# Attention events in order of time, and weight sums made in place at one pair in three steps

## The chip, the cores and the metric

The kernel runs on one core of a Trainium2 chip. The metric is the device time of one execution in microseconds (us), the median of several runs. Beside it stands one profiled execution, whose trace gives every instruction's start, duration and wait. The engines are named as in the profile: PE is TensorE (PEld its weight loads), DVE is VectorE, ACT is ScalarE, POOL is GpSimd, SP is SyncE, which here only issues DMAs.

## What is computed

Attention in a sliding window of 64 keys, over 8 sequences of 576 tokens with 8 heads of 64 channels, and behind it a feed-forward layer (512 to 2048 to 512) with the Mish function. All of it is float32.

```python
scores = scale * np.matmul(q, k.transpose(0, 1, 3, 2))
mask = (rel >= 0) & (rel < window)          # window = 64
scores = np.where(mask, scores, -1000000000.0)
scores = scores - np.max(scores, axis=-1, keepdims=True)
attn = np.exp(scores)
attn = attn / (np.sum(attn, axis=-1, keepdims=True) + 1e-09)
x = np.matmul(attn, v)                      # then heads side by side: 4608 x 512
h = x @ w_in
sp = np.where(h > 20.0, h, np.log1p(np.exp(np.minimum(h, 20.0))))
out = (h * np.tanh(sp)) @ w_out
```

## The kernel before

**Tiling.** The 4608 tokens are 12 chunks of 384. The attention of a chunk is four units `p`, one for each pair of heads (`NPAIR`). The feed-forward layer of a chunk is 16 steps `f` of 128 hidden channels. To keep float32 accuracy, each operand is split into a high and a low part in float32r, and each product is three matmuls (high by high, high by low, low by high). The high and low parts of the first weight lie in the tile `wi`, those of the second in `wo_h` and `wo_l`.

**Plain stage.** Chunks 0 to 3 are computed step by step (`steps`, a list of 64 pairs of chunk and `f`; indices 32 to 47 are chunk 2, 48 to 63 chunk 3). A step is twelve matmuls into `h_ps` on PE (called H below), two Mish activations on ACT (`t`, `gh`), a subtraction on POOL (`gl`), and, two steps later, nine matmuls into the three `acc` banks (called A below).

**Attention beside it.** While PE runs the steps of one chunk, the attention of a later one is put between them. For chunk 3 this is a list of events (time in half steps, kind, function, unit) that `Att.plan` fills at line 546: scores at `begin + p * step`, transposition 0.6 of a step later, values 1.5 steps later (`lag=1.5`, line 768). `run(slot)` (line 549) takes events from the front of the list while the first one is due. These lie within chunk 2's steps. A unit's path is: score matmuls into `s_ps` (PE; called S), masks (DVE, `pr<-s_ps,masks`), a table load and six exponentials (ACT, `pr<-pr,mx`), normalisation and a 32-by-32 transposition (DVE, `sm`, `pr`, `tr`), twelve DMAs that move blocks of `tr` to their place in `pT` (SP, `pT<-tr`), value matmuls into `o_ps` (PE; called O), and the split of the result on ACT (`xh`) and DVE (`xl`).

**Wide stage.** Chunks 4 to 11 are computed two at a time (`Wide`), with seven products of sums of weight blocks and activation blocks in place of eight products. Its attention (`Wide.run`, line 842) computes the values of unit `k - 1` (matmuls into `at`) beside the scores of unit `k` (into `s_ps` and `at`) in one place; `first_runs` puts runs 0 to 4 of the first pair of chunks among chunk 3's steps. Its transposed probabilities `tr` have the buffer `st0` (line 881).

**Weight sums.** For each pair `g` of hidden blocks, `make_sums` (line 788) forms four sums of weight blocks and writes them, split, to `sums` in DRAM: plain blocks are copied by DMA (lines 791, 792), `w` is the sum of the high and low parts (DVE, line 796, buffer `st0`), `s` holds the four sums (DVE, line 803, buffer `st1`), and `two` holds high and low parts of two of them at a time (ACT line 807, POOL line 808, buffers `st2` and then `st0`), from which one DMA for each two sums writes them (line 809). A manual dependency keeps the start of each behind the PE instruction that was last in program order. The loop at line 1123 calls it at steps with `n % 4 == 1`: 33, 37, ... 61. `load_sums` later brings the sums of a pair from DRAM into a ring that lies over `wi`; `Wide.fills` (line 909) splits the activation sums into slots that also lie over `wi` (ACT line 906, DVE line 907, with POOL's subtractions at line 915). `kept["u"]`, which the first product of each wide pair is copied to (ACT, line 966), has the buffer `st2`.

**What sets the order.** Each engine executes its instructions in the order of its queue. Up to step 31 the program order is kept; from there a scheduler orders the instructions of DVE, ACT, POOL and SP by dependencies and priorities when the kernel is built. SP's queue holds all loads of q, k and v, the moves `pT<-tr` and the writes of `sums`, and a DMA that waits holds up all that stand behind it.

Of the kernel before, what the change touches and what calls it, by code (L numbers as in the profile page):

```python
# [10 lines left out]
F32 = mybir.dt.float32  # L11
F32R = mybir.dt.float32r
# [3 lines left out]
ALU = mybir.AluOpType  # L16

P = 128
# [11 lines left out]
def tile_window_attn_mish_ffn(  # L30
# [10 lines left out]
    nc = tc.nc  # L41
# [15 lines left out]
    NG = NF // 2  # L57
# [51 lines left out]
    def thin_masks(engine):  # L109

        for r in range(TQ, P, BLK):
            for k in range(0, TK, TQ):
                engine.tensor_copy(all_masks[r:r + TQ, :, k:k + TQ], all_masks[r:r + TQ, :, k + TQ:k + 2 * TQ])
# [7 lines left out]
    wi = const.tile([P, NF, 2, NC_, P], F32R, name="wi")  # L121
# [12 lines left out]
    def in_order():  # L134
        return tc.issue_after(order[-1]) if order else nullcontext()
# [20 lines left out]
    def st_home(shape, dtype, name, n=None):  # L156
        return mp.tile(shape, dtype, name=name, tag=f"st{next(st_turn) if n is None else n}", bufs=1)
# [270 lines left out]
    def w_ready(piece):  # L428

        lo, hi, wh, wl = piece  # L430
        vec.tensor_scalar(lo, lo, 29, None, ALU.logical_shift_right)
        yield
        vec.tensor_scalar(hi.bitcast(F32), hi.bitcast(F32), BIG, -BIG, ALU.min, ALU.max)
        yield

    def w_joined(piece):

        lo, hi, wh, wl = piece
        vec.scalar_tensor_tensor(lo, hi, 3, lo, ALU.logical_shift_left, ALU.bitwise_or)
        yield  # L440
        vec.scalar_tensor_tensor(lo, hi, 0x80000000, lo, ALU.bitwise_and, ALU.bitwise_or)
        rounding.append(lambda copy: copy(wh, lo.bitcast(F32)))
        yield

    def w_rest(piece):
        lo, hi, wh, wl = piece
        vec.tensor_tensor(wl, lo.bitcast(F32), wh.bitcast(F32), ALU.subtract)
        w_load()
        yield
# [98 lines left out]
    events = []  # L548
    def run(slot):
        while events and events[0][0] <= slot:  # L550
            _, _, fn, p = events.pop(0)
            fn(p)
# [4 lines left out]
    def flush():  # L557
        c, f, gg = pend.pop(0)
        if f == 0:
            if c == 1:  # L560
                accs[c] = [at_bank(f"acc1_{t}", DO) for t in range(NTT)]
            else:
                accs[c] = [ps_acc.tile([P, DO], F32, name=f"acc{t}", tag=f"acc{t}") for t in range(NTT)]
        ffn_out(accs[c], gg, f)
        if f == NF - 1:
            ffn_store(c, accs.pop(c))
# [12 lines left out]
    starts = {c: 2 * len(steps) + 2 * NF * (c - 2) for c in range(2, PLAIN + 1)}  # L579
# [49 lines left out]
    def step(n, h_ps=None):  # L629
        pend.append((*steps[n], function(h_ps or first_half(n))))  # L630
# [58 lines left out]
    parts = {}  # L689
# [76 lines left out]
    ahead = 6  # L766
    begin = starts[2] + ahead - 1
    atts[3].plan(begin, (starts[3] - ahead - begin) / (NPAIR + 0.5), lag=1.5)
    begin = starts[3] - ahead

    PIECE = 2 * 2 * P
    RING = NPROD * PIECE
    sums = tc.dram_tile([NG, P, RING], F32, name="sums")
# [5 lines left out]
    def piece(g, m):  # L779

        def at(first, order="p (l k n) -> p l k n"):
            return ring[:, g % 2, first * PIECE:(first + 1) * PIECE].rearrange(order, l=2, k=2)
        if m in (A11, A12):
            both = ring[:, g % 2, :2 * PIECE].rearrange("p (l h k n) -> p l h k n", l=2, h=2, k=2)
            return both[:, :, m == A12]
        return at({S2: 2, S3: 3, A22: 4, S1: 5, S4: 6}[m])

    def make_sums(g):

        f0, f1 = 2 * g, 2 * g + 1  # L790
        kept_ = [nc.sync.dma_start(sums[g, :, :2 * PIECE], wi[:, f0].rearrange("p l c n -> p (l c n)").bitcast(F32)),
                 nc.sync.dma_start(sums[g, :, 4 * PIECE:5 * PIECE].rearrange("p (l n) -> p l n", l=2),
                                   wi[:, f1, :, 2:, :].rearrange("p l c n -> p l (c n)").bitcast(F32))]
        w = st_home([P, 2, 2, 2 * P], F32, "w", 0)
        parts = [wi[:, f0:f1 + 1, i, :, :].rearrange("p f c n -> p f (c n)").bitcast(F32) for i in range(2)]
        kept_.append(nc.vector.tensor_tensor(w.rearrange("p f h n -> p f (h n)"), *parts, ALU.add))
        for i in kept_:
            tc.add_manual_dep(i.ins, order[-1].name, SYNC, reason="the steps before it first")
        s = st_home([P, 4, 2 * P], F32, "s", 1)
        s1, s2, s3, s4 = (s[:, i, :] for i in (2, 0, 1, 3))  # L800
        for out_, a, b, op in ((s1, w[:, 1, 0, :], w[:, 1, 1, :], ALU.add), (s2, s1, w[:, 0, 0, :], ALU.subtract),
                               (s3, w[:, 0, 0, :], w[:, 1, 0, :], ALU.subtract), (s4, w[:, 0, 1, :], s2, ALU.subtract)):
            nc.vector.tensor_tensor(out_, a, b, op)
        for n, first in ((2, 2), (0, 5)):
            two = st_home([P, 2, 2, 2 * P], F32R, "two", n)
            i = slice(0, 2) if n else slice(2, 4)
            nc.scalar.copy(two[:, :, 0, :], s[:, i, :])
            nc.gpsimd.tensor_tensor(two[:, :, 1, :], s[:, i, :], two[:, :, 0, :].bitcast(F32), ALU.subtract)
            nc.sync.dma_start(sums[g, :, first * PIECE:(first + 2) * PIECE],
                              two.rearrange("p m l n -> p (m l n)").bitcast(F32))  # L810

    def load_sums(g, part):
        g %= NG
        nc.scalar.dma_start(ring[:, g % 2, part].bitcast(F32), sums[g, :, part])
# [231 lines left out]
    def weights(n):  # L1046
        for i in range(5 + (n in MORE)):
            if i == RES:
                residue()
            next(ops, None)  # L1050

    def some_moves():
        if slow:
            each, moved = slow.pop(0)
            moved.extend(itertools.islice(each, 4))

    def between(n):

        if n in SCORES:
            p = SCORES.index(n)  # L1060
            third.products(p, [h_bank("s_ps") for _ in range(2)])
            third.load(p + 2, "qk")
            with in_order():
                flush()
            third.masked(p, BY_HEAD, exps=False)
            if p % 2:
                third.exp(p - 1)
                third.exp(p)
        if n - 1 in SCORES[1::2]:
            third.normal(SCORES.index(n - 1) - 1)  # L1070
        if n - 2 in SCORES[1::2]:
            third.normal(SCORES.index(n - 2))
        if n in MOVED:
            p = MOVED.index(n)
            third.dve_transpose(p, p > 1)

    sums_made = 0
# [5 lines left out]
    def wide_runs(slot):  # L1083
        while first_runs and first_runs[0][0] <= slot:
            with in_order():
                wides[0].run(first_runs.pop(0)[1])

    for n, (c, f) in enumerate(steps):
        held[0] = n < starts[2] // 2
        if n >= starts[2] // 2 and f == 0:  # L1090

            while any(fn.__self__ is atts[c] for _, _, fn, _ in events):
                run(events[0][0])
        if n == starts[2] // 2:
            held[0] = True
            third.values(NPAIR - 1, h_bank)
            with in_order():
                flush()
            held[0] = False
        if n >= HEAD:  # L1100
            step(n)
        if n == MASKED:
            thin_masks(pool)
        run(2 * n)
        wide_runs(2 * n)
        if held[0]:
            if n not in SCORES:
                weights(n)
            if last < n < last + NPAIR:
                third.values(n - last - 1, h_bank)  # L1110
        if len(pend) > LAG:
            with in_order():
                flush()
        if held[0]:
            between(n)
            if n in SCORES:
                weights(n)
            some_moves()
            if last - 2 <= n < last:
                third.load(n - last + 2, "v")  # L1120
        run(2 * n + 1)
        wide_runs(2 * n + 1)
        if n >= starts[2] // 2 and n % 4 == 1 and sums_made < NG:
            make_sums(sums_made)
            sums_made += 1
        if c == PLAIN - 1 and f in (7, 8):
            for part in LOADS:
                load_sums(f - 7, part)
# [77 lines left out]
```

## Time and profile before

| | |
|---|---|
| Time, median of 3 runs | 945.4 us (944.63 to 946.57) |
| The profiled execution | 947.67 us, of which the span from the first to the last instruction is 945.8 us |
| PE busy | 879.3 us (93% of the span) |
| DVE, ACT, POOL busy | 440.5, 459.8, 240.1 us |
| Mean granted TensorE clock | 0.969 |

An engine is busy while an instruction of it executes; waiting in front of one is idle time, and the trace names for each idle stretch the event that came last before the instruction (its releaser). The granted clock is the share of TensorE's full rate that the chip allowed in a stretch; 1.00 and 0.50 are its two levels here (2.4 and 1.2 GHz). Times in rows are from the start of the span.

### The profile page before, as it was taken

What the parts mean: (1) busy time and instruction counts of PE and PEld (TensorE: products, weight loads), DVE (VectorE), ACT (ScalarE), POOL (GpSimd) and SP (SyncE); (2) the same over time, 40 slices, a digit from 0 to 9 for tenths busy, and PEclk for the clock granted to TensorE, in tenths of its full rate; (3) what the DMA queues carried; (4) which work ended last, traced back from release to release, by engine and by line L of the source; (5) the groups of instructions that cost most, each with busy time, mean ns of one, the idle gap of its engine ahead of it and who ended that gap; (6) DMA issues with size and microseconds to landing.
All of it is one profiled execution on the core that took longest, in us unless ns stands there. A gap on an engine that the chain in (4) does not pass through costs nothing.

```text
span 945.8 us, 18947 instructions
## 1 busy us (share of the span) xinstructions
PE 879.3 (93%) x7162; PEld 778.8 (82%) x7162; DVE 440.5 (47%) x1271; ACT 459.8 (49%) x1215; POOL 240.1 (25%) x227
## 2 busy tenths in 40 slices
PE   7899999997796887499999999999999999999998
PEld 6788888896686876478988888888888988898987
DVE  7887986332242436344245544245544244332322
ACT  6767464454552654255347455346455344332322
POOL 4400000233121235221314312315311324322221
PEclk8999999998898998699999999999999999999999
DMA  9554543452556654375555565555575543533311
GB/s 306 169 171 134 159 155 113 151 190 62 170 158 224 232 168 155 118 222 156 177 171 183 160 227 155 177 171 185 161 224 154 176 137 123 178 123 112 123 34 67
DMA packets 91771, 152.05 MB, mean 161 GB/s; under 512 B 9760, under 2 KB 72736, under 8 KB 87584
## 3 DMA queue, kind: packets, MB, share of 16 engines
q1 hardware_dynamic: 77424, 84.31, 28.1%
q10 hardware_dynamic: 14256, 66.53, 21.9%
q8 instruction: 57, 0.93, 0.4%
q14 instruction: 34, 0.28, 0.1%
HBM read 114.88 MB, written 24.12 MB: 147 GB/s over the span
## 4 chain that ended last, share of the span: by engine, by line
PE 55%; DMA 4%; DVE 4%; ACT 3%; issue 2%; SPq 2%; POOL 0%; ACTq 0%; DVEq 0%; POOLq 0%
PE acc L129 27%; PE m_ps L129 23%; DMA sums<-two 3%; PE at L129 3%; ACT pr L82 2%; DVE wi L907 2%; SPq L82 2%; PE s_ps L129 2%; DMA out<-o 1%; PE h_ps L129 1%; DVE sm L82 1%; DVE pr L82 1%; ACT xn L865 0%; DMA pT<-tr 0%; DVE tr L82 0%
## 5 line engine op out<-in xcount | busy, mean ns | idle before, releaser
L129 PE MATMUL m_ps<-wi 128*128 128x384 f32 x1152 | 221.7, 340 | 24.1 <-ACT u L966 19.7
L129 PEld LDWEIGHTS m_ps<-wi 128*128 128x128 f32 x1152 | 204.2, 189 | 37.3 <-ACT u L966 21.0
L129 PE MATMUL acc<-wo_h,gh 128*128 128x512 f32 x576 | 227.9, 400 | 7.1 <-ACT o L383 7.1
L947 POOL TENSOR_TENSOR gl<-t,gh 128x384 fp32r<-128x384 f32 x128 | 131.4, 1027 | 383.4 <-PE m_ps L129 122.5
L129 PE MATMUL acc<-wo_l,gh 128*128 128x512 f32 x576 | 226.8, 394 | 0.0
L129 PE MATMUL acc<-wo_h,gl 128*128 128x512 f32 x576 | 224.3, 392 | 0.0
L129 PE MATMUL h_ps<-xh,wi 128*128 128x384 f32 x512 | 143.3, 342 | 0.4 <-ACT pT L82 0.4
L129 PEld LDWEIGHTS acc<-wo_h,gh 128*128 128x128 f32 x576 | 108.6, 189 | 26.7 <-ACT o L383 7.5
L129 PEld LDWEIGHTS acc<-wo_h,gl 128*128 128x128 f32 x576 | 108.7, 189 | 24.9
L129 PEld LDWEIGHTS acc<-wo_l,gh 128*128 128x128 f32 x576 | 109.0, 189 | 15.5
L82 ACT ACTIVATE pr<-pr,mx 128x96 f32<-128x96 f32 (+1 forms) x288 | 105.6, 372 | 19.9 <-DVE mx L82 19.7
L942 ACT ACTIVATE gh<-t 128x384 fp32r<-128x384 f32 x96 | 50.4, 526 | 125.8 <-DVE t L959 84.9
L959 DVE TENSOR_TENSOR u<-u,m_ps 128x384 f32<-128x384 f32 x64 | 35.3, 552 | 140.2 <-PE m_ps L129 135.8
L129 PEld LDWEIGHTS h_ps<-xh,wi 128*128 128x128 f32 x512 | 95.2, 191 | 4.0 <-ACT pT L82 0.6
L959 DVE TENSOR_TENSOR t<-u,m_ps 128x384 f32<-128x384 f32 x96 | 53.1, 553 | 84.3 <-PE m_ps L129 84.3
L129 PE MATMUL h_ps<-xl,wi 128*128 128x384 f32 x256 | 87.0, 340 | 0.0
L82 POOL TENSOR_TENSOR gl<-t,gh 128x384 fp32r<-128x384 f32 x32 | 34.9, 1090 | 180.4 <-ACT gh L82 166.7
L82 DVE CUSTOM_DVE_ANT_0 pr<-s_ps,masks 128x96 f32<-128x96 f32 (+1 forms) x256 | 49.6, 259 | 62.7 <-PE s_ps L129 59.6
L82 ACT ACTIVATE t<-h_ps 128x384 f32<-128x384 f32 x64 | 31.5, 492 | 69.7 <-PE h_ps L129 67.1
L82 ACT ACTIVATION_READ_ACCUMULATOR pr<-pr,mx 128x1 f32 x288 | 55.2, 192 | 0.0
L1032 DVE TENSOR_TENSOR acc_sb<-acc_sb,acc 128x512 f32<-128x512 f32 x56 | 38.4, 686 | 34.8 <-PE acc L129 34.8
L943 ACT ACTIVATE t<-t 128x384 f32<-128x384 f32 x96 | 50.2, 525 | 8.7 <-PE m_ps L129 0.5
(72 smaller groups left out, 942.2 us busy)
## 6 DMA issues: line engine op xcount, KB each, us to landing
wi<-sums ACTq DMA_DIRECT2D x32, 1024.0 KB, 5.2
wi<-sums ACTq DMA_DIRECT2D x32, 768.0 KB, 4.8
v_t<-vN SPq DMA_DIRECT2D x46, 384.0 KB, 4.6
k_t<-kT SPq DMA_DIRECT2D x44, 224.0 KB, 5.2
pT<-tr SPq DMA_DIRECT2D x192, 48.0 KB, 3.5
q_t<-qT SPq DMA_DIRECT2D x47, 192.0 KB, 5.1
st<-w_in SPq DMA_DIRECT2D x16, 512.0 KB, 3.6
st<-w_out SPq DMA_DIRECT2D x16, 512.0 KB, 3.6
```

The source lines that it names most:

```text
L82: i = call(*args, **kw)
L129: i = nc.tensor.matmul(*args, **kw)
L907: nc.vector.tensor_tensor(low, b, high.bitcast(F32), ALU.subtract)
L942: nc.scalar.activation(gh, t, AF.Mish)
L943: nc.scalar.activation(t, t, AF.Mish)
L947: nc.gpsimd.tensor_tensor(gl, t, gh.bitcast(F32), ALU.subtract)
L959: nc.vector.tensor_tensor(out_, a, b, ALU.add)
L1032: nc.vector.tensor_tensor(total, total, acc, ALU.add)
```

## The change

It has three parts. The list of events is sorted by time and kind, so that the scores of unit `p + 1` (at 1.0 step behind those of `p`) are taken from the list ahead of the values of unit `p` (at 1.5). `make_sums` forms the four sums in the tile that holds the parts: `w` has the buffer `st1`, all four high parts go into one tile `high` in `st2` with one ACT instruction, the low parts overwrite `w` with one POOL instruction, and each of the two tiles is written with one DMA, in runs of 256 elements (1 KB) where before a run had 1024 (4 KB); two places of the ring change names accordingly. And the pairs are made at steps 33, 36, 39, ... 54.

```diff
     atts[3].plan(begin, (starts[3] - ahead - begin) / (NPAIR + 0.5), lag=1.5)
+    events.sort(key=lambda e: e[:2])
     begin = starts[3] - ahead
...
-        return at({S2: 2, S3: 3, A22: 4, S1: 5, S4: 6}[m])
+        return at({S2: 2, S3: 3, S4: 4, S1: 5, A22: 6}[m])
...
-                 nc.sync.dma_start(sums[g, :, 4 * PIECE:5 * PIECE].rearrange("p (l n) -> p l n", l=2),
+                 nc.sync.dma_start(sums[g, :, 6 * PIECE:].rearrange("p (l n) -> p l n", l=2),
                                    wi[:, f1, :, 2:, :].rearrange("p l c n -> p l (c n)").bitcast(F32))]
-        w = st_home([P, 2, 2, 2 * P], F32, "w", 0)
-        parts = [wi[:, f0:f1 + 1, i, :, :].rearrange("p f c n -> p f (c n)").bitcast(F32) for i in range(2)]
-        kept_.append(nc.vector.tensor_tensor(w.rearrange("p f h n -> p f (h n)"), *parts, ALU.add))
+        w = st_home([P, 4, 2 * P], F32, "w", 1)
+        parts = [wi[:, f0:f1 + 1, i, :, :].rearrange("p f (h k) n -> p f h (k n)", h=2).bitcast(F32) for i in range(2)]
+        kept_.append(nc.vector.tensor_tensor(w.rearrange("p (h f) n -> p f h n", h=2), *parts, ALU.add))
         for i in kept_:
             tc.add_manual_dep(i.ins, order[-1].name, SYNC, reason="the steps before it first")
-        s = st_home([P, 4, 2 * P], F32, "s", 1)
-        s1, s2, s3, s4 = (s[:, i, :] for i in (2, 0, 1, 3))
-        for out_, a, b, op in ((s1, w[:, 1, 0, :], w[:, 1, 1, :], ALU.add), (s2, s1, w[:, 0, 0, :], ALU.subtract),
-                               (s3, w[:, 0, 0, :], w[:, 1, 0, :], ALU.subtract), (s4, w[:, 0, 1, :], s2, ALU.subtract)):
+        a11, a21, a12, a22 = (w[:, i, :] for i in range(4))
+        for out_, a, b, op in ((a22, a21, a22, ALU.add), (a21, a11, a21, ALU.subtract),
+                               (a11, a22, a11, ALU.subtract), (a12, a12, a11, ALU.subtract)):
             nc.vector.tensor_tensor(out_, a, b, op)
-        for n, first in ((2, 2), (0, 5)):
-            two = st_home([P, 2, 2, 2 * P], F32R, "two", n)
-            i = slice(0, 2) if n else slice(2, 4)
-            nc.scalar.copy(two[:, :, 0, :], s[:, i, :])
-            nc.gpsimd.tensor_tensor(two[:, :, 1, :], s[:, i, :], two[:, :, 0, :].bitcast(F32), ALU.subtract)
-            nc.sync.dma_start(sums[g, :, first * PIECE:(first + 2) * PIECE],
-                              two.rearrange("p m l n -> p (m l n)").bitcast(F32))
+        high = st_home([P, 4, 2 * P], F32R, "high", 2)
+        nc.scalar.copy(high, w)
+        low = w.bitcast(F32R)
+        nc.gpsimd.tensor_tensor(low, w, high.bitcast(F32), ALU.subtract)
+        for i, part in enumerate((high, low)):
+            to = sums[g, :, 2 * PIECE:6 * PIECE].rearrange("p (m l n) -> p m l n", m=4, l=2)
+            nc.sync.dma_start(to[:, :, i, :], part.bitcast(F32))
...
-        if n >= starts[2] // 2 and n % 4 == 1 and sums_made < NG:
+        if n >= starts[2] // 2 and (n - starts[2] // 2) % 3 == 1 and sums_made < NG:
```

**First place: ACT's queue in chunk 2's steps, from the exponentials of unit 1.** ACT has one instruction for each thing that PE does there: `pr,sm<-pr,mx` (six) follows a unit's scores, `t` and `gh` follow each H, `xh<-o_ps` follows a unit's values. Before:

```order
L82 CAST xh1_2463<-o_ps_2465 128x384
L807 CAST two_2440<-s_2431 128x2x256
L82 ACT_TABLE_LOAD
L82 ACTIVATE pr_2508,sm_2510<-pr_2508,mx_2509 128x96 x6
L82 ACT_TABLE_LOAD
L82 ACTIVATE t_2566<-h_ps_2553 128x384
L82 ACTIVATE gh_2567<-h_ps_2553 128x384
L82 ACTIVATE t_2594<-h_ps_2581 128x384
L82 ACTIVATE gh_2595<-h_ps_2581 128x384
L82 CAST xh1_2463<-o_ps_2609 128x384
```

The values of unit 0 (`o_ps_2465`) stand ahead of the exponentials of unit 1, and two H lie between those and the values of unit 1 (`o_ps_2609`). In the changed kernel:

```order
L82 ACTIVATE pr_2453,sm_2455<-pr_2453,mx_2454 128x96 x6
L82 ACT_TABLE_LOAD
L82 ACTIVATE t_2497<-h_ps_2484 128x384
L82 ACTIVATE gh_2498<-h_ps_2484 128x384
L82 CAST xh1_2503<-o_ps_2505 128x384
L82 ACTIVATE t_2558<-h_ps_2545 128x384
L82 ACTIVATE gh_2559<-h_ps_2545 128x384
L82 ACT_TABLE_LOAD
L82 ACTIVATE pr_2599,sm_2601<-pr_2599,mx_2600 128x96 x6
L82 ACT_TABLE_LOAD
L82 ACTIVATE t_2647<-h_ps_2634 128x384
L82 ACTIVATE gh_2648<-h_ps_2634 128x384
```

Behind the exponentials of unit 1 now come the values of unit 0 (`o_ps_2505`) and the exponentials of unit 2; those of unit 1 stand two rows further. On PE three H, four A, the values of unit 0 and the scores of unit 2 lie between the scores and the values of unit 1.

**Second place: SP's queue at the moves of unit 3 of chunk 3.** Before:

```order
L809 DMA sums<-two 128x1024 x2
L82 DMA v_t<-vN 128x6x128
L82 DMA q_t<-qT 128x384
L82 DMA k_t<-kT 128x448
L82 DMA pT<-tr 32x192 x12
```

In the changed kernel:

```order
L82 DMA pT<-tr 32x192 x2
L82 DMA v_t<-vN 128x6x128
L82 DMA pT<-tr 32x192 x3
L810 DMA sums<-high 128x4x256
L82 DMA pT<-tr 32x192 x3
L810 DMA sums<-w 128x4x256
L82 DMA pT<-tr 32x192 x4
```

The twelve moves stood in one piece; a load of v, which waits for the values of unit 2, and both writes of a pair's sums, which wait for ACT and for POOL, now stand among them. Units 2 of chunk 3 and 1 of the first wide pair also have sums among their moves, the others none.

**Third place: DVE's queue at the end of chunk 3.** `tr` are the transposed probabilities of the next wide pair of chunks, L907 the low parts of the activation sums, `u` the first addition of the wide stage. Before:

```order
L907 TENSOR_TENSOR x_4225<-xn_3805,x_4225 128x768
L82 STREAM_TRANSPOSE tr<-pr 128x6x3x32 x2
L796 TENSOR_TENSOR w<-wi 128x1024
L803 TENSOR_TENSOR s<-w 128x256 x2
L907 TENSOR_TENSOR wi<-t_4226,wi 128x768
L803 TENSOR_TENSOR s<-s,w 128x256
L907 TENSOR_TENSOR wi<-t_4227,wi 128x768
L803 TENSOR_TENSOR s<-w,s 128x256
L959 TENSOR_TENSOR u<-u,m_ps 128x384 x2
```

In the changed kernel:

```order
L907 TENSOR_TENSOR wi<-xn_3258,wi 128x768
L82 TENSOR_TENSOR pr<-pr,sm 128x576
L82 STREAM_TRANSPOSE tr<-pr 128x6x3x32
L907 TENSOR_TENSOR x_4193<-xn_3807,x_4193 128x768
L907 TENSOR_TENSOR wi<-t_4195,wi 128x768
L959 TENSOR_TENSOR u<-u,m_ps 128x384 x2
```

The last pair's `w` and its four sums are gone from here; they now stand ahead of the scores of the first wide pair's unit 3.

## Rows read from the trace of the kernel before

**Rows 1.** The page, part 1: busy us (share of the span) xinstructions.

```profile
PE 879.3 (93%) x7162; PEld 778.8 (82%) x7162; DVE 440.5 (47%) x1271; ACT 459.8 (49%) x1215; POOL 240.1 (25%) x227
```

**Rows 2.** PE's waits from 177 to 391 us: total us, times, longest.

```profile
PE m_ps L129 <- ACT u L966: 18.4, 1, 18.4
PE o_ps L129 <- DMA pT<-tr: 12.7, 3, 6.0
PE acc L129 <- ACT o L383: 7.1, 1, 7.1
PE at L129 <- DMA pT<-tr: 5.5, 2, 3.0
PE s_ps L129 <- ACT gh L82: 1.4, 1, 1.4
```

**Rows 3.** Windows at half clock: length; PE, PEld, DVE, ACT, POOL busy; PEclk; DMA; GB/s.

```profile
219.20:225.90 6.70, 5.91 (x82) 5.54 (x83) 1.92 (x15) 4.02 (x14) 0.00 (x0) 0.50 0.43 110
249.90:256.60 6.70, 3.75 (x121) 3.38 (x121) 0.88 (x4) 1.78 (x3) 0.00 (x0) 0.50 0.18 49
287.50:294.10 6.60, 3.09 (x9) 2.80 (x10) 2.56 (x5) 2.63 (x4) 1.00 (x1) 0.50 0.73 267
328.40:331.60 3.20, 3.20 (x83) 3.08 (x82) 2.84 (x15) 2.48 (x12) 0.00 (x0) 0.50 0.45 131
352.30:359.00 6.70, 5.02 (x68) 4.36 (x69) 4.93 (x22) 4.36 (x19) 0.55 (x2) 0.50 0.55 154
390.60:396.40 5.80, 5.80 (x17) 5.41 (x18) 1.09 (x2) 0.87 (x2) 1.00 (x1) 0.50 0.11 25
```

**Rows 4.** The chain that ended last: start, us, what; one H and one A.

```profile
297.61 2.08 PE h_ps L129 x12
299.70 2.06 PE acc L129 x9
```

**Rows 5.** Timeline of PE, unit 1 of chunk 3: start, us, instruction [idle before <-releaser].

```profile
203.68 0.83 PE L129 MATMUL s_ps<-k_t,q_t 64*32 64x96 f32 x48
...
219.99 1.55 PE L129 MATMUL o_ps<-pT,v_t 128*64 128x64 f32 x24 [4.88 <-DMA pT<-tr]
```

**Rows 6.** Timeline of SP, the same unit's moves.

```profile
210.93 7.50 SPq L82 DMA_DIRECT2D pT<-tr  x12
```

**Rows 7.** Timeline of ACT at the end of chunk 2.

```profile
286.64 1.58 ACTq L388 DMA_DIRECT2D out<-o  x2
288.31 1.28 ACT L82 ACT_TABLE_LOAD   x1 [4.37 <-DMA sums<-two]
```

**Rows 8.** DVE's waits from 177 to 391 us.

```profile
DVE tr L82 <- DMA sums<-two: 11.2, 3, 5.6
```

**Rows 9.** Timelines of four engines at the end of chunk 3.

```profile
367.97 2.56 POOL L915 TENSOR_TENSOR t<-xn,t 128x768 f32<-128x768 f32 x1
...
368.75 2.59 DVE L907 TENSOR_TENSOR x<-xn,x 128x768 fp32r<-128x768 f32 x1
371.26 1.43 DVE L82 STREAM_TRANSPOSE tr<-pr 128x576 f32<-128x576 f32 x2
...
372.72 7.48 SPq L82 DMA_DIRECT2D pT<-tr  x12
...
381.73 1.23 DVE L796 TENSOR_TENSOR w<-wi 128x1024 f32<-128x1024 f32 x1 [9.04 <-DMA pT<-tr]
...
383.67 0.95 DVE L907 TENSOR_TENSOR wi<-t,wi 128x768 fp32r<-128x768 f32 x1
...
387.31 1.54 SPq L809 DMA_DIRECT2D sums<-two  x2
...
390.07 0.48 ACT L966 COPY u<-m_ps 128x384 f32<-128x384 f32 x1 [3.21 <-DMA sums<-two]
```

**Rows 10.** POOL's group of low parts (count, busy, mean ns), and landing of `sums` writes.

```profile
L808 POOL TENSOR_TENSOR two<-s,two 128x512 fp32r<-128x512 f32 x16 | 20.9, 1326 | 24.1 <-issue 18.8 <-DMA v_t<-vN 5.2
...
DMA to landing us min/median/max: 2.6/5.1/9.7
```

## The prediction

> **What bounds the kernel now.** I read the shares of the page first: PE is busy for 93% of the span and no other engine for half of it [rows 1], so work taken from DVE, ACT or POOL is worth nothing by itself; what can be won is PE's idle time and the clock that PE gets. PE's waits by releaser came next. In the stretch that the change touches, 177 to 391 us, five groups of waits add up to 18.4 + 12.7 + 7.1 + 5.5 + 1.4 = 45.1 us [rows 2]. Then the windows with the granted clock: in the same stretch six windows ran at 0.50, and PE was busy in them for 5.91 + 3.75 + 3.09 + 3.20 + 5.02 + 5.80 = 26.8 us [rows 3]. One H takes 2.08 us and one A 2.06 at full clock [rows 4]; work that takes 26.8 us at half clock would take about 13.4, so some 13.4 us are lost there (an estimate, since a matmul's time need not be exactly halved). Last I read the timelines around the largest waits; they name the mechanism of each, below.
>
> **Part 1, the sorted events (o_ps, 12.7 us idle in three waits).** Unit 1 of chunk 3 shows how a unit runs: scores begin at 203.68, values at 219.99, so its path through masks, exponentials, transposition and moves takes 16.3 us, of which PE idles 4.88 at the end [rows 5]. PE has S + 3 A + 2 H between the two, 0.83 + 3 x 2.06 + 2 x 2.08 = 11.2 us, and that is too little. With the sorted list three H, four A, the values of unit 0 and the scores of unit 2 lie there. The values took 1.55 us at half clock [rows 5], so about 0.8 at full. The work becomes 0.83 + 4 x 2.06 + 3 x 2.08 + 0.8 + 0.83 = 16.9 us, more than the 16.3 of the path: no wait. For unit 2 the order gives the same 16.9, for unit 3 about 16.1.
>
> What speaks against zero is SP's queue. The twelve moves of a unit take 7.50 us to issue [rows 6] and now have a pair's sums among them at units 2 and 3; two writes of sums took 1.54 us to issue [rows 9]. At unit 3 ten moves also stand behind a load of v that waits for the values of unit 2. From there: 10/12 x 7.50 = 6.3, one or two writes 0.8 to 1.5, a last move's landing of about 1.8 (an estimate: the path of unit 1 ends at 219.99, its last issue at 210.93 + 7.50 = 218.4, [rows 5, 6]), together 8.9 to 9.7 against 2 H + 2 A = 8.3 us of PE work. So unit 3 waits 0.6 to 1.4, unit 2 about 0.4 to 1.6 for the same writes. I take 3.0 us for the group (bounds 0, if the moves find the queue free, and 8, if unit 3 also waits for POOL's new instruction and a landing).
>
> **Part 2, sums in place (m_ps 18.4, at 5.5).** At the end of chunk 3 the transposed probabilities and `w` share one buffer. The trace shows a single file: `tr` at 371.26, its moves from 372.72 to 380.20, and only then the last pair's `w` at 381.73, after 9.04 us of waiting for them; behind it stand two of DVE's fills of the slots (the first at 383.67); then `two`, the write at 387.31, and ACT's copy `u`, which waits 3.21 us for that write since it overwrites `two` [rows 9]. PE gets its product at 390.60 [rows 3], 18.4 us after it ran out of work at 372.2 [rows 2]. In the new order the last pair is made at step 54 instead of 61, and nothing of it stands here. What is left ahead of `u` is POOL's `t`, done at 367.97 + 2.56 = 370.53, one fill of 0.95 and the copy of 0.48 [rows 9]: 372.0, about when PE arrives. I take 1.0 us of wait (bounds 0, and 5 if DVE's three fills of up to 2.59 us follow one another behind POOL).
>
> `tr` waited 11.2 us in three places for writes of sums [rows 8]; with separate buffers these waits go, and the units of the wide pair begin their moves that much sooner. The two waits `at <- pT` of 5.5 us [rows 2] are behind those. I leave 2.0 (bounds 0 and 6), since unit 1 of the wide pair now has sums among its moves.
>
> The added cost: DVE, ACT and POOL handle the same elements. ACT's 16 casts become 8 of twice the size, POOL's 16 of 1.33 us [rows 10] become 8 of about 2.65 (an estimate by size). They have over half of their time free [rows 1] and `gl` is needed only two steps later, so I cost them at nothing; without that cover, the 1.3 us by which one is longer would be paid at eight pairs, 10 us. The writes have four times as many runs of a quarter the length. Their landing took 2.6 to 9.7 us, median 5.1 [rows 10]; no row here tells what 1 KB runs do to it, so the bounds are these two ends, and I take the median. It matters in one place: `w` and `high` have one home each, so DVE's `w` of a pair waits for the landing of the pair before. The path from one `w` to the next is about 1.2 for `w`, 1.9 for the sums, 1.2 for ACT, 2.65 for POOL, 0.4 for the issue, and 5.1: 12.5 us (from the durations of [rows 9, 10] and by size). Three steps are 3 x (2.08 + 2.06) = 12.4 and scores and values come on top, so this just passes.
>
> DVE's fill `x<-xn,x` takes 2.59 us where POOL's `t` of 2.56 runs beside it, and a fill of the same size takes 0.95 where POOL is idle [rows 9]: the two engines hold each other up. The Trainium skill, page "SBUF — State Buffer", section "Who interferes with whom", has a rule for it: VectorE and GpSimd share one pair of ports under an exclusive lock, so one that needs it waits until the other is done. The trace agrees in direction. By this rule POOL's doubled instruction could hold a two-operand instruction of DVE 1.3 us longer; at the three units that have a pair's sums beside their transposition that would be 4 us, and the time about 905.
>
> **Part 3, one pair in three steps (acc 7.1, s_ps 1.4).** PE waits 7.1 us for ACT's evacuation of chunk 2's output [rows 2]. ACT's issue of `out<-o` begins at 286.64, and a table load follows 4.37 us late for a write of sums, in a window where the DMA engines are 0.73 busy [rows 3, 7]. With other steps and other buffers that write is elsewhere: 7.1 - 4.4 = 2.7, taken as 2.8 (bounds 0.5 and 7.1, if another transfer is as late). The wait of 1.4 for ACT's `gh` I put at 0.4 (bounds 0 and 1.4).
>
> **Sum.** Idle left: 1.0 + 3.0 + 2.8 + 2.0 + 0.4 = 9.2, so 45.1 - 9.2 = 35.9 us are gained. The half-clock windows begin at PE's longer waits; the 1.4 us wait for `gh` has none [rows 2, 3]. Of the waits that I leave two may come as single waits above 2 us, so I leave two windows of average size, 26.8 / 6 = 4.5 us busy each, which lose 4.5 in all: 13.4 - 4.5 = 8.9 gained. Together 44.8. From 391 us on PE is the bound and nothing is changed, so the gain reaches the end. The profiled execution took 947.67, so 947.67 - 44.8 = 902.9; the median of the runs is 2.3 below that execution, which gives 900.6, **901 us**. With all lower bounds (0.5 us idle, no half clock) it is 945.4 - 44.6 - 13.4 = 887; with the upper ones (27.5 idle, all half clock kept) 928.
>
> **Rivals.**
> 1. The moves are held up behind the sums. SP executes in order, and at three units the sums' writes wait for ACT and POOL among the moves. For it: the queue's order in the changed kernel; PE's margin is 0 to 0.6 us. Against: the sums are begun well ahead of the moves. Price: 3.5 us more at three places and two half-clock windows more, 10.5 + 4.5 = 15, so 916 (912 to 925).
> 2. The last fill at the start of the wide stage comes late, because POOL, ACT and DVE still do it one after another. Half of the 18.4 stays, 9.2 - 1.0 = 8.2, and a window of 5.80 keeps 2.9 [rows 3]: 912.
> 3. Slower than before: DVE's `w` waits for the landing of the pair before, and stands ahead of masks and of the evacuation of `acc` in DVE's queue, so PE stops. The path without its landing is 12.5 - 5.1 = 7.4 us and three steps are 12.4, so each landing L beyond 5.0 stops PE for L - 5.0, at seven pairs; and each stop brings a half-clock window of 4.5 us busy, 2.2 lost, 7 x 2.2 = 16 less the 4.5 counted already, 11 in all. It decides the sign from 7 x (L - 5.0) + 11 = 44.8, L = 9.8, the slowest landing of before [rows 10]. With 11 us, which the shorter runs could make of it, 42 + 11 = 53 is lost: 954. Against it: 9.7 was one landing, not the median, in the stretch with the busiest DMA.
> 4. The change doesn't do what it says: PE, not these buffers, releases the waits, or they are replaced by equal ones from POOL or SP. Then 945. Against it: DVE's 9.04 and ACT's 3.21 name the shared buffers directly [rows 9].
>
> **How the numbers follow.** The forecast gets 0.67, with a range of its own of 893 to 912; the first rival 0.22, the second 0.06, the third 0.03, the fourth 0.02. To leave out no more than 2 in 10 the range takes in the second rival and most of the first, and comes near the lower bound: 890 to 920. About 0.2% (1.9 us) can be told from no change here. Faster by more than that are the forecast and the first two rivals, 0.95; the same is the fourth, 0.02; slower the third, 0.03.
>
> **What would show it.** Right: PE's wait for `u` at the start of the wide stage below 5 us, no wait of `tr` for writes of sums, no wait of unit 1's values, at most three half-clock windows between 177 us and the start of the wide stage, and PE's first product of that stage near 346 us (390.6 - 44.8). Wrong: waits `o_ps <- pT` or `at <- pT` of 3 us or more with `sums` issued late among the moves (rival 1); DVE's `w` waiting for `sums` with `s_ps` or `acc` waiting for DVE (rival 3); a new wait at `acc` as long as the old, which would mean that the transfers and not the sums' buffers held ACT.

## The result and the profile after

The changed kernel takes 911.0 us (median of 4 runs, 910.21 to 918.31) where the kernel before took 945.99 beside it: ratio 0.9641, 95% interval 0.9592 to 0.9691. Measured again on another occasion it took 913.46 against 946.93: 0.9629 (0.9609 to 0.9650). So the change wins 33 to 35 us where 44.8 were forecast: the time is inside the predicted range of 890 to 920 and 10 to 12 us above the forecast of 901.

The first profiled execution of the changed kernel is the slowest of its runs (918.31, span 916.5), so the profile of the second measurement (913.8, span 912.0) stands beside it below.

PE's waits in the stretch that the change touches, first profile (total us, times, longest); they answer to [rows 2]:

```profile
PE at L129 <- DMA pT<-tr: 5.7, 1, 5.7
PE o_ps L129 <- DMA pT<-tr: 5.7, 2, 3.2
PE acc L129 <- ACT o L383: 2.8, 1, 2.8
PE m_ps L129 <- DVE u L959: 1.1, 1, 1.1
PE m_ps L129 <- ACT u L966: 0.9, 1, 0.9
```

The same of the second profile:

```profile
PE o_ps L129 <- DMA pT<-tr: 4.9, 2, 3.2
PE acc L129 <- ACT o L383: 2.8, 1, 2.8
...
PE at L129 <- DMA pT<-tr: 0.2, 1, 0.2
```

The wait of 18.4 us for `u` is gone. The waits for the moves are what remains, and one of them, 5.7 us at the wide pair's unit 1, is in the first profile and nearly absent (0.2) from the second; why is shown below. Unit 1 of chunk 3, the example of the prediction, no longer waits; units 2 and 3 do. The group of twelve matmuls that PE began at 390.60 before (it is the second group of the wide stage) begins at 360.99 and 355.50; the prediction named 346.

Half clock, windows of the second profile (columns as in [rows 3]): two of them, 12.0 us busy, where [rows 3] has six with 26.8.

```profile
244.40:251.20 6.80, 6.07 (x126) 5.22 (x127) 2.78 (x25) 4.10 (x15) 0.00 (x0) 0.50 0.44 127
278.50:285.30 6.80, 5.98 (x17) 5.59 (x18) 0.03 (x1) 2.04 (x4) 3.37 (x2) 0.50 0.80 287
```

For a balance I cut the execution at two instructions that every one of these kernels has: the one place near 177 us where two H follow each other directly, and the 25th matmul into `m_ps`, after the first two groups of twelve of the wide stage. Windows of the kernel before, from the one to the other and from there to the end (columns as above):

```profile
176.76:396.92 220.16, 175.02 (x1660) 155.81 (x1659) 81.86 (x279) 104.31 (x292) 65.21 (x53) 0.88 0.50 161
396.92:945.80 548.88, 536.34 (x4111) 476.38 (x4109) 222.40 (x604) 245.73 (x626) 152.18 (x139) 1.00 0.50 157
```

The same of the changed kernel, first profile:

```profile
177.80:365.90 188.10, 171.20 (x1661) 151.21 (x1659) 81.45 (x279) 103.50 (x284) 62.54 (x45) 0.95 0.59 186
365.90:916.50 550.60, 536.83 (x4111) 476.89 (x4109) 222.46 (x604) 245.77 (x626) 152.15 (x139) 1.00 0.48 157
```

And second profile:

```profile
178.33:360.41 182.08, 169.78 (x1660) 149.75 (x1659) 79.80 (x279) 103.42 (x284) 62.16 (x45) 0.96 0.60 192
360.41:912.00 551.59, 536.64 (x4111) 476.67 (x4109) 222.65 (x604) 245.63 (x626) 152.44 (x139) 1.00 0.49 157
```

Idle time is length less PE's busy time. The gain against the kernel before, in us:

| | predicted | first profile | second profile |
|---|---|---|---|
| idle time of the stretch (45.1 before) | 35.9 | 28.2 | 32.8 |
| busy time of the stretch (175.0 before) | 8.9 | 3.8 | 5.2 |
| ahead of the stretch | 0 | -1.0 | -1.6 |
| behind it | 0 | -1.7 | -2.7 |
| sum | 44.8 | 29.3 | 33.8 |

### The profile page after: what moved, and what is told of

Same layout as the page of the kernel before. It is cut to its first block, busy times and chain, and to the rows that moved or that the text cites. A ratio compares the mean times of both kernels' runs of the same rounds, so it can differ in the third digit from the quotient of the medians.

```text
span 916.5 us, 18893 instructions
## 1 busy us (share of the span) xinstructions
PE 877.5 (96%) x7162; PEld 776.0 (85%) x7162; DVE 440.0 (48%) x1271; ACT 459.1 (50%) x1207; POOL 237.8 (26%) x219
## 4 chain that ended last, share of the span: by engine, by line
PE 82%; DVE 6%; DMA 4%; ACT 4%; SPq 2%; issue 1%; POOL 0%; ACTq 0%; POOLq 0%; DVEq 0%
PE acc L129 39%; PE m_ps L129 23%; PE h_ps L129 13%; PE s_ps L129 3%; PE at L129 3%; ACT pr L82 2%; SPq L82 2%; DVE wi L907 2%; PE o_ps L129 1%; DMA pT<-tr 1%; DVE pr L82 1%; DMA sums<-wi 1%; DMA wi<-sums 1%; DVE sm L82 1%; DMA k_t<-kT 1%
```

## The experiments

**The three parts, alone and in pairs.** I call sorting the events S, sums in place in other buffers B, and the pace of one pair in three steps R. First each alone, and S with B.

```diff
# S alone, on the kernel before
+    events.sort(key=lambda e: e[:2])
# B alone: the changed kernel without the line above, and
-        if n >= starts[2] // 2 and (n - starts[2] // 2) % 3 == 1 and sums_made < NG:
+        if n >= starts[2] // 2 and n % 4 == 1 and sums_made < NG:
# R alone: on the kernel before, the last two lines the other way round
# S with B: the changed kernel with only the last two lines
```

S alone, expected: 

> The kernel before with only the events sorted. Theory of the prediction (each part pays for its own group of waits): o_ps falls from 12.7 us in three waits to 3 to 6, since sums still stand among the moves of two units; the 18.4 us at the start of the wide stage and the 7.1 at acc stay; with 1 to 3 us of clock some 9 us are gained, 936 (933 to 940). Rival (a unit's path is held up by the sums among its moves as long as before, so a wait only moves to another place): 943 to 948.

B alone, expected: 

> The kernel before with only the sums in place, in other buffers; pairs still at every fourth step, the last at 61. Theory A (the shared buffers made the 18.4 us): the first product of the wide stage waits 6 us or less, tr no longer waits for writes of sums, time 928 (924 to 933). Theory B (the late last pair made it: even in other buffers its high parts lie where the copy u has to go, so u waits for the landing of their write): 9 us or more of the 18.4 stay, time 934 to 942.

R alone, expected: 

> The kernel before with only the pairs at steps 33, 36, ... 54; one buffer is still shared by w, two and tr. Theory A (shared buffers): tr still waits 8 us or more for writes of sums, at <- pT grows to 8 us or more, m_ps keeps 5 us or more of its 18.4: 935 (930 to 940). Theory B (the late last pair): the 18.4 us fall below 3 with nothing else done, 924 (920 to 929), though tr waits for writes of sums as before.

S with B, expected: 

> The changed kernel with pairs at every fourth step as before (sorted events and sums in place stay). Theory A: m_ps below 6 us, acc waits about 7 again: 917 (913 to 921). Theory B: 9 us or more of the wait at the start of the wide stage stay, 924 to 932.

Then the two pairs that were missing, by the same edits.

B with R, expected: 

> The changed kernel without the sorted events (sums in place, one pair in three steps). The sort alone won 11.4 us. Theory H (the parts add): o_ps waits of 12 to 13 us are back and the kernel is about 11 us slower than the changed one, 923 (920 to 926). Theory I (with the sums out of the way a unit's path is short enough): o_ps below 8 us and the time under 919.

S with R, expected: 

> The changed kernel with the sums formed in separate buffers as before, one of them shared with tr (sorted events, one pair in three steps). Theory J (either the pace or the buffers is enough for the wait at the start of the wide stage, and the buffers alone also free tr): m_ps below 3 us, but tr waits 8 us or more for writes of sums and at <- pT is 5 us or more: 922 (917 to 927). Theory K (the two parts add): 10 us or more at the start of the wide stage, 930 or more.

S with B again, and the changed kernel again, side by side:

> The changed kernel with pairs at every fourth step, beside the changed kernel on the same chip. Theory C (the faster pace wins nothing once the buffers are apart): within 2 us of the changed kernel or below it. Theory D (the equality of the last two medians is chance; the prediction gave the pace some 6 us): 4 to 6 us above the changed kernel.

> The changed kernel once more, as the common measure for the runs of this call. All theories: 911 (908 to 915), with PE's waits o_ps and at for the moves as in its first profile, 13 us in all; if the 5.7 us wait at <- pT of that profile comes from one slow landing among the moves, it may be 2 us smaller here and the time 2 us with it.

Measured (ratio to the kernel before measured beside it, 95% interval; PE's waits in the stretch in us, m_ps those for `u` on ACT and DVE, at those for moves and "issue"):

| kernel | median us | ratio | o_ps | m_ps | acc | at |
|---|---|---|---|---|---|---|
| before | 945.4 | 1 | 12.7 | 18.4 | 7.1 | 5.5 |
| S | 937.22 | 0.9881 (0.9860 to 0.9901) | 5.5 | 19.4 | 5.9 | 4.7 |
| B | 923.89 | 0.9747 (0.9721 to 0.9774) | 12.7 | 4.1 | 6.9 | 2.0 |
| R | 935.03 | 0.9859 (0.9829 to 0.9888) | 12.5 | 1.3 | 4.3 | 8.9 |
| S, B | 910.73 | 0.9607 (0.9582 to 0.9632) | 2.7 | 3.5 | 2.0 | 0.9 |
| S, B again | 913.73 | 0.9642 (0.9625 to 0.9659) | 4.5 | 3.2 | 2.0 | 1.8 |
| B, R | 929.12 | 0.9788 (0.9761 to 0.9815) | 11.9 | 1.6 | 4.4 | 3.4 |
| S, R | 927.19 | 0.9765 (0.9742 to 0.9788) | 4.2 | 1.4 | 5.6 | 10.5 |
| S, B, R (the change) again | 913.46 | 0.9629 (0.9609 to 0.9650) | 4.9 | 2.0 | 2.8 | 1.2 |

What follows:
- S and B add: 0.9881 x 0.9747 = 0.963, and 0.9607 and 0.9642 are measured. S takes most of the o_ps waits away wherever it stands (2.7 to 5.5 us are left), and neither of the others does (11.9 to 12.7 without it).
- The wait at the start of the wide stage has two sufficient cures. B alone leaves 4.1 us though the last pair is still made at step 61 (theory A); R alone leaves 1.3 though the buffer is still shared (theory B). Each theory had the wait right on its own kernel and wrong on the other's; in time, theory B missed its own kernel (935, not 924), since with R alone the waits `at` and `s_ps` grow (5.5 to 8.9 and 1.4 to 4.4). Both causes were needed for the 18.4 us: a buffer shared with `tr` and a pair late enough to meet it. B joins two things, other buffers and forming the sums in place with half as many instructions; that it is the buffers is read from the waits of [rows 8, 9], and no run separates the two.
- R wins 13.6 us alone (948.65 before, measured beside it) and nothing beside S and B (913.46 and 913.73 side by side: theory C). Beside B it seems to cost some 4 us: B with R is at 0.9788 against 0.9747 for B alone, with intervals that overlap a little.
- The wait at acc does not need R: S with B have 2.0 at the old pace. My expectation of 7 there was wrong; why S and B shorten it was not isolated.
- Two expected times were clearly missed: S with B came out below its range (910.73, 913 at least expected), since acc did not come back, and B with R above it (929.12, 926 at most), though its o_ps waits are as theory H has them; the reason follows. B alone and S with R lie 0.1 and 0.2 us outside theirs. The change again had 6.1 us at o_ps and at where 13 were expected.

What R brings beside B is in the profile of B with R. First PE's waits there:

```profile
PE o_ps L129 <- DMA pT<-tr: 11.9, 3, 5.7
PE h_ps L129 <- DVE mx L82: 7.4, 1, 7.4
```

The second is new. DVE's timeline of the same kernel around it (start, us, instruction, idle before and releaser):

```profile
281.63 1.23 DVE L796 TENSOR_TENSOR w<-wi 128x1024 f32<-128x1024 f32 x1 [16.98 <-DMA sums<-w]
...
284.61 0.25 DVE L82 CUSTOM_DVE_ANT_0 pr<-s_ps,masks 128x96 f32<-128x96 f32 x1
```

and the landing of the four writes of `sums` that SP issues from 271.5 to 273.2 us, and of a load of the ring that ACT issues among them:

```profile
DMA to landing us min/median/max: 6.2/9.4/9.8
```

`w` has one home and waits for the write of the pair before, which was issued at 272.1 and took over 9 us to land; the masks stand behind `w`, and PE waits 7.4 us for them. This is the prediction's third rival, with its mechanism, its place and about its landing, in one pair instead of seven. The changed kernel has the same wait of DVE, 8.53 us, but with the sorted events only the next sums stand behind it and no masks:

```profile
285.66 1.23 DVE L797 TENSOR_TENSOR w<-wi 128x1024 f32<-128x1024 f32 x1 [8.53 <-DMA sums<-w]
286.92 2.65 DVE L803 TENSOR_TENSOR w<-w 128x256 f32<-128x256 f32 x4
291.97 0.26 DVE L82 CUSTOM_DVE_ANT_0 pr<-s_ps,masks 128x96 f32<-128x96 f32 x1 [2.39 <-PE s_ps L129]
```

**The waits for the moves that are left.** SP's queue of the changed kernel, first profile, at unit 3 of chunk 3 and at unit 1 of the wide pair:

```profile
232.80 1.88 SPq L82 DMA_DIRECT2D pT<-tr  x2
234.78 0.53 SPq L82 DMA_DIRECT2D v_t<-vN  x1
...
240.66 2.75 SPq L82 DMA_DIRECT2D pT<-tr  x4
...
279.37 2.23 SPq L82 DMA_DIRECT2D pT<-tr  x3
281.70 0.53 SPq L810 DMA_DIRECT2D sums<-w  x1
282.27 9.26 SPq L82 DMA_DIRECT2D pT<-tr  x9
```

Unit 3's moves take from 232.80 to 243.41, 10.6 us instead of the 7.50 of [rows 6], as the order said. SP's waits from 231 to 245 us come to 0.3 us in all, so nothing holds the queue there; it is full of issues:

```profile
SPq L82 <- DVE w L803: 0.3, 1, 0.3
```

At the wide unit nine moves take 9.26 us, though twelve took 7.48 [rows 9]. SP's waits from 276 to 292 us name the reason:

```profile
SPq L82 <- DMA wi<-sums: 3.4, 1, 3.4
```

A move waits 3.4 us for a load of the ring, issued on another queue, that has nothing to do with its data: a wait that no buffer explains. (In the built program the DMAs use eight semaphores in turn, and each waits for the one that had its semaphore before. That this is the reason here is read from the program; no run changes it.)

What PE waits for at the end is the landing of the last move. SP issues it at 290.95, just behind another load of the ring that ACT issues; PE starts only when it has landed:

```profile
290.80 0.33 ACTq L814 DMA_DIRECT2D wi<-sums  x1
...
297.64 2.83 PE L129 MATMUL at<-pT,v_t 128*64 128x64 f32 x48 [5.74 <-DMA pT<-tr]
```

In the second profile the same load goes out at 293.29, after the last move (issued by 292.41), and PE starts at 294.32 with next to no wait. So most of the 5.7 us is one slow landing, as the expectation for the repeated run had it.

The next kernels put the moves in one piece, by a high priority for the scheduler, once at either pace:

```diff
-                yield load.dma_start(pT[k:k + TQ, r // TQ, :, :], tr[r:r + TQ, i, :, :])
+                with tc.high_priority(offset=SOON):
+                    d = load.dma_start(pT[k:k + TQ, r // TQ, :, :], tr[r:r + TQ, i, :, :])
+                yield d
...
-                    moves.append(load.dma_start(pT_all[at:at + TQ, r // TQ].rearrange("p u j q -> p (u j q)"),
-                                                tr[r:r + TQ, i].rearrange("p u j q -> p (u j q)")))
+                    with tc.high_priority(offset=SOON):
+                        moves.append(load.dma_start(pT_all[at:at + TQ, r // TQ].rearrange("p u j q -> p (u j q)"),
+                                                    tr[r:r + TQ, i].rearrange("p u j q -> p (u j q)")))
```

One pair in three steps, expected: 

> The changed kernel with a high priority for the moves, so that the scheduler puts all twelve moves of a unit in one piece ahead of the sums. Theory E (the sums and the load of v among the moves make the o_ps and at waits that are left): these 13 us fall below 5, the time by 6 to 10 us under the changed kernel, 903. Theory F (the waits are the path through masks, exponentials and twelve issues of 0.6 us, whatever stands among them): they stay above 9 us and the time within 2 us of the changed kernel.

One pair in four steps, expected: 

> The same priority with pairs at every fourth step. Theory E: little to win, since few sums stand among the moves at this pace: o_ps and at waits of 2 to 4 us, the time 0 to 3 us under that of the changed kernel with every fourth step, 907. Theory F: no difference to it.

and again, beside the next kernel: 

> The kernel with the moves in one piece and pairs at every fourth step once more, as the measure for the next run: 907 (905 to 910). One at wait of 2 to 4 us, no o_ps wait above 1.

Measured beside the changed kernel (913.46): 914.03 at three steps (ratio 0.9644, 0.9626 to 0.9662) and **907.1 at four** (0.9581, 0.9558 to 0.9604); again, later, 908.22 (0.9570, 0.9545 to 0.9595). At three steps the o_ps waits fall from 4.9 to 1.8 us as theory E has it, but the at waits grow, so the time stays: E's number for the time failed. F's two numbers hold (the time within 2 us, the waits above 9), but not its reason, since the o_ps waits did answer to what stands among the moves. At four steps E's 907 was met. PE's waits at three steps:

```profile
PE at L129 <- DMA sums<-w: 5.6, 1, 5.6
PE at L129 <- DMA pT<-tr: 3.8, 1, 3.8
PE o_ps L129 <- DMA pT<-tr: 1.8, 1, 1.8
```

and at four, second time, where nothing above 2.2 us is left in the stretch:

```profile
PE m_ps L129 <- ACT u L969: 2.2, 1, 2.2
```

The 5.6 us at three steps are not the order of SP's queue. All twelve moves are issued in one piece there, from 255.65 to 263.42, but in the middle of them ACT issues a load of the ring:

```profile
255.65 7.77 SPq L82 DMA_DIRECT2D pT<-tr  x12
...
260.33 0.35 ACTq L816 DMA_DIRECT2D wi<-sums  x1
```

The landing of the seven moves issued up to then (first row), and of the last five (second):

```profile
DMA to landing us min/median/max: 1.9/1.9/2.8
...
DMA to landing us min/median/max: 4.2/5.1/5.8
```

So a move that starts beside that load lands some 3 us later (median 5.1 against 1.9). The Trainium skill, page "DMA: Bandwidth & Descriptors", section "Queues, rings and completion order", says that SP's and ACT's queues are rings on the same 16 engines; these rows agree.

The other part of the 5.6 us is the third rival again. The unit's last exponential ends at 247.75, but DVE begins its normalisation (`sm`) at 250.12, since `w` stands ahead of it and waits for the landing of a write:

```profile
248.98 1.22 DVE L799 TENSOR_TENSOR w<-wi 128x1024 f32<-128x1024 f32 x1 [3.82 <-DMA sums<-w]
250.12 0.98 DVE L82 TENSOR_SCALAR sm<-sm 128x6 f32<-128x6 f32 x1
```

These 2.4 us and the 3 of the landings are about the 5.6; no run separates them.

**Loads of the ring later**, on the kernel with the moves in one piece and four steps:

```diff
-        if c == PLAIN - 1 and f in (7, 8):
+        if c == PLAIN - 1 and f in (10, 11):
             for part in LOADS:
-                load_sums(f - 7, part)
+                d = load_sums(f - 10, part)
+                tc.add_manual_dep(d.ins, order[-1].name, SYNC, reason="the steps before it first")
```

Expected: 

> The kernel with the moves in one piece and every fourth step, in which the four loads of the ring are held until steps 58 and 59 of the plain stage; they went at steps 47 to 53 before. Theory L (what is left of the at wait are moves that land in 3 to 6 us instead of 1.9 while such a load of 0.75 or 1 MB runs): at waits below 2 us and the time 1 to 4 us lower, 905. Theory M (the loads are not what slows the moves): the at waits stay and the time is the same within 1 us, or higher if the first product of the wide stage waits for its load.

Measured: 916.78 (0.9653, 0.9629 to 0.9676), against 908.22 measured beside it. PE's waits:

```profile
PE m_ps L129 <- ACT u L969: 11.0, 1, 11.0
PE at L129 <- DMA pT<-tr: 4.1, 1, 4.1
```

The at wait of 0.6 and 3.9 us at about 306 in the two profiles with the early loads is gone; one of 4.1 us stands at 331, where the loads now run; the moves issued beside them took, from issue to landing,

```profile
DMA to landing us min/median/max: 4.1/6.0/7.3
```

That moves land late beside the loads (theory L) is thereby seen a second time; that this shift wins time is refuted. The loads only meet the next unit, ACT stands 6.0 us behind them in its own queue, and the old wait is back in a new form: `high` lies where `u` goes, and ACT's copy waits for its write.

```profile
ACT u L969 <- DMA sums<-high: 8.8, 1, 8.8
ACT t L82 <- DMA wi<-sums: 6.0, 1, 6.0
```

Most of the 8.8 us is not landing. ACT had `high` ready at 350.96, but the write stands behind twelve moves in SP's queue and goes out at 356.31:

```profile
348.73 7.48 SPq L82 DMA_DIRECT2D pT<-tr  x12
356.31 0.53 SPq L812 DMA_DIRECT2D sums<-high  x1
```

## Why the prediction was right, and where its sizes were off

**Right: the direction, the range and the main mechanisms.** The sorted events removed unit 1's wait by the work that they put between its scores and values, and S is the only part that does so. The separate buffers removed the 18.4 us: B alone takes it to 4.1. No wait of `tr` for writes of sums is left in the changed kernel, while S with R, which shares the buffer, has 15.3 us of them in three places. Of the prediction's signs of being right only the start of the stage at 346 us failed; but one of its signs for the first rival showed too (3.2 us at `o_ps` with sums among the moves), so 911 lies in the range with a part of that rival in it.

**Idle time, 35.9 forecast and 28.2 to 32.8 found.** The terms that were left, forecast against the two profiles: m_ps 1.0 against 2.0 and 2.0; acc 2.8 against 2.8 and 2.8; s_ps 0.4 against 0 and 1.0; o_ps 3.0 against 5.7 and 4.9 (5.4 with 0.5 that DVE's `w` released); at 2.0 against 6.3 and 1.2. The mis-sized step is the one on SP's queue. The working took the issue times of the writes among the moves and gave unit 3 0.6 to 1.4 us; it measured 3.2:

```profile
232.23 0.92 PE L129 MATMUL o_ps<-pT,v_t 128*64 128x64 f32 x24 [2.50 <-DMA pT<-tr]
...
244.89 1.54 PE L129 MATMUL o_ps<-pT,v_t 128*64 128x64 f32 x24 [3.21 <-DMA pT<-tr]
```

Two terms were too small. The working let v's load go out when unit 2's values end, at 233.15; it went at 234.78, 1.6 us later, because SP was still issuing. And the load, ten moves and two writes took SP 8.6 us (234.78 to 243.41), not 7.1 to 7.8. The rest held: PE starts 1.5 us after the last issue (1.8 allowed), and its work between the two units is 8.5 us (8.3). At the wide unit 1 the step left out what is shown above: a move that waits for a load of the ring (3.4 us), and one that lands late beside such a load. That is the first rival in weaker form and with another cause, full queues and loads in place of writes that wait: it gave 916, and 911 and 913 lie between it and the forecast.

**The clock, 8.9 forecast and 3.8 to 5.2 found.** The number of windows was about right: two and three, 12.0 and 15.5 us busy, where 9.0 were forecast. The price was wrong. From the balance, 3.8 us were won for 26.8 - 15.5 = 11.3 us busy fewer at half clock, and 5.2 for 14.7: 0.34 to 0.36 us for each, not 0.5. The kernel with the moves in one piece and four steps gives the same (175.02 - 169.17 = 5.85 for 26.8 - 9.0 = 17.8, 0.33). At 0.35 the 26.8 us were worth 9.4, not 13.4. The working had named the halving as an estimate; it nearly holds for groups like H. The twelve matmuls that begin at 390.60 in the kernel before are followed by the next group at 394.60, 4.0 us later, where H, of the same size, takes 2.08 [rows 4]; but a unit's values took 0.92 us at full clock in the kernel before

```profile
202.84 0.92 PE L129 MATMUL o_ps<-pT,v_t 128*64 128x64 f32 x24
```

and 1.55 at half [rows 5], a loss of 0.63 / 1.55 = 0.4. The scores lose least: 48 take 0.83 us at full clock [rows 5], 0.0173 each, and in a half-clock window of the first profile 80 take 1.85, 0.0231 each, a loss of a quarter:

```profile
246.37 1.85 PE L129 MATMUL s_ps<-k_t,q_t 64*32 64x96 f32 x80
```

Four of the six windows of [rows 3] hold 68 to 121 matmuls and two hold 9 and 17, so the four are full of these small ones.

**Behind the stretch, 0 forecast and -1.7 to -2.7 found.** The step "from 391 us on PE is the bound and nothing is changed" failed. The long wait had also given the next unit's moves time: before, they were issued by 380.20 [rows 9] and the values ran at 401.56; now they are issued by 363.68 and PE stands ready at 365.11, so the values come 1.8 us too late, the second wait below. PE's waits of the second profile behind the stretch:

```profile
PE m_ps L129 <- DVE u L959: 4.5, 4, 2.5
...
PE at L129 <- DMA pT<-tr: 1.8, 1, 1.8
```

The kernel before has no wait `at` behind its stretch, and 3.3 us of the first in four, with 1.2 as the longest (first profile: 3.5 and 1.3); why one of them is 2.5 here stays open. Ahead of the stretch nothing is changed; its 1.0 to 1.6 us are the run's own (the first cut lies between 176.4 and 179.2 us in the profiles of this study).

**Wrong in its attribution: part 3.** The working credited the pace with 4.3 us at acc and 1.0 at s_ps. Undone in the changed kernel, the pace is worth nothing, and acc is shorter without it (2.0). That acc came out at the forecast 2.8 is luck: the reason given for it was not the cause.

**The rule on the shared ports** would have cost 4 us. POOL's new instruction takes 2.39 us, near the estimate by size (2.65), but no such price shows: DVE's `pr<-pr,sm`, the two-operand instruction ahead of each transposition, takes 0.75 to 0.76 us in 12 of its 14 places in the stretch, in both profiles, and the two long ones (2.1 and 2.4) stand beside POOL's `xn`, `t` and `gl`, not beside this instruction. So this is not where the missing 10 us went.

```profile
L807 POOL TENSOR_TENSOR w<-w,high 128x1024 fp32r<-128x1024 f32 x8 | 19.1, 2386 | 3.2 <-ACT high L805 2.8 <-PE acc L129 0.4
```

## What to carry to other kernels

When a wait has two causes, a shared buffer and a late producer say, either cure may do, and parts of a change that each win alone need not add: price each beside the others. Look for what a wait's end releases: when 18 us of idle time go, the transfers that used them as cover show up next. On a queue that also moves small blocks on the path, keep those in one piece: here that, at the old pace, gave 907 to 908 us, 6 us better than the change, and nothing at the new pace. It has a price, since what stands behind the piece waits for it. Large transfers of other queues beside such blocks make them land late, but moving those loads to a later place lost 8.6 us here.

## What the runs showed of the hardware

- A fall of the clock to half costs matmuls unequally: twelve matmuls of 128x384 take 4.0 us against 2.08, the small matmuls of the values lose 0.4 of their time at half clock, those of the scores a quarter, and the stretch as a whole 0.33 to 0.36 us for each us that PE is busy at half clock.
- A move of 48 KB lands in 1.9 us with no load beside it and in 4 to 7 us beside a load of 0.75 or 1 MB that another engine issued.
- Writes in runs of 1 KB did not land later than those of 4 KB, all of 512 KB: the sixteen of the changed kernel take 3.2, 4.3 and 6.4 us (least, median, most) in the first profile and 3.1, 4.7 and 8.1 in the second, where [rows 10] has 2.6, 5.1 and 9.7, and S with R, with runs of 4 KB at the same pace, 2.9, 4.3 and 7.1.
